# A kernel of attention and feed-forward: the order of all units of work as a written table in place of a list scheduler

## The chip, the cores and the metric

The kernel runs on one core of a Trainium2 chip. The metric is the device time of one execution in microseconds (us), the median of three runs. The engines are named as in the profile: PE (TensorE, products), PEld (its weight loads), DVE (VectorE), ACT (ScalarE), POOL (GpSimd), and SP (SyncE), which issues every DMA of this kernel.

## The reference

Clustered attention is followed by a feed-forward layer with a maximum of three branches. Four batches, 8 heads, 768 positions, 64 wide; 16 clusters; the layer is 512 to 768 to 512 for 3072 tokens, all in float32.

```python
q_assign = np.argmax(np.einsum('bhsd,hcd->bhsc', q_n, c_n), axis=-1)   # q_n, k_n, c_n: rows divided by their norm
k_assign = np.argmax(np.einsum('bhsd,hcd->bhsc', k_n, c_n), axis=-1)
mask = q_assign[:, :, :, None] == k_assign[:, :, None, :]
scores = np.where(mask, scale * np.matmul(q, k.transpose(0, 1, 3, 2)), -1000000000.0)
attn = softmax(scores)                       # maximum taken off, exp, divided by the sum
x = np.matmul(attn, v)                       # heads side by side: 3072 x 512
h = np.maximum(np.maximum(x @ w1, x @ w2), x @ w3)
out = h @ w_out
```

## The kernel before

Float32 values are split into a high and a low float16 part, so that a product of two such values is three products in float16. Heads go in pairs (4 pairs in each of 4 batches). The kinds of work are:

- *prep(b, pr)*: q and k of a pair are loaded (L678) into a stage buffer, scaled by a power of two that comes from their maximum (L684 or L686, then small DVE steps L692 to L715 and a small product, L702), and split (L753 to L761). Cluster scores (L734 in batch 0, L778 and L782 later) are transposed on DVE (L530), turned into one-hot rows (L533 to L579), and moved into the operands, so that one product gives the score and the mask.
- *v_first, v_prep*: the same for v (L838 to L904); the maximum over the partitions goes through a small product (L425).
- *weights*: w1, w2, w3 and w_out arrive as 64-bit numbers (wd, L961), are cast and shifted to float32 (L966 or L968, L972), scaled by their maximum (L1013), and split into w16a, w16b and wo (L983 to L989).
- *tile_units*: the 192 tiles of 128 queries by 768 keys: scores on PE (L1203, L1205) into a PSUM tile called big, row maximum on DVE (L1214), exponential on ACT (L1220), the split (L1223 or L1276, then L1226 or L1279), and the transposition of both parts by DMA (L1229). In the first 40 tiles every second one is transposed by PE instead (L1251, taken out by L1257 and L1259).
- *visit*: six tiles make a visit (three of each head); then the product with v (L1153). In batch 0 the sums are divided out afterwards: L1138, L1145, spread by ACT (L1168), multiplied by DVE (L1172) and split (L929 or L931, L1087).
- *ffn*: when the four pairs of a block of 384 tokens are there, 18 hidden products (L1335) of 12 matmuls, evictions with the maximum (L1347, L1349), splits (L929 or L931, L1087), then 3 output products (L1388), eviction and store (L1398, L1402).

A *unit* is one step of these kinds: a function that issues one or a few instructions on one engine. `Plan.add` collects 3117 of them with their dependences, their buffers (*leases*) and a priority. A unit whose engine is a dict (`pick`) may run on one of several: 640 units. `port=True` marks work on DVE which the scheduler keeps apart from work on POOL.

`Plan.run` of before is a list scheduler. It keeps a clock per engine, and takes on each free engine the ready unit of the lowest priority, moved by constants in NUDGE. For a `pick` unit it chooses the engine that would end first. The order in which units are taken is the order in which their instructions are issued, so it fixes the queue of every engine. Between engines, the framework puts the semaphores. All buffers of a tag come from one pool with `bufs` places.

```python
if u.pick and min(u.costs, key=lambda x: over(u, x)) != e:
    continue
late = max(u.at, when) + self.SAFE[e] > now
if rank is None or (late, u.prio, u.n) < rank:
    best, rank = u, (late, u.prio, u.n)
```

Of the kernel before, what the change touches and what calls it, by code (L numbers as in the profile page):

```python
# [8 lines left out]
F32 = mybir.dt.float32  # L9
# [13 lines left out]

class Lease:
    def __init__(self, plan, tag, make):
        self.tag, self.make, self.users, self.held, self.tile = tag, make, [], False, None
        plan.leases.append(self)

    def __call__(self):
        if self.tile is None:  # L30
            self.tile = self.make()
        return self.tile
# [12 lines left out]
class Plan:  # L45


    LAG = {"PE": 0.17, "DVE": 0.085, "ACT": 0.09, "POOL": 0.03, "SP": 0.0}
    SEM = 0.04
    LAND = 1.45  # L50
    RING = 2.6
    NEAR = 0.0
    SAFE = {"PE": 0.5, "DVE": 0.0, "ACT": 0.0, "POOL": 0.0, "SP": 0.0}
    BIAS = {"PE": 0.0, "DVE": 0.5, "ACT": 0.0, "POOL": 0.0, "SP": 0.0}

    def __init__(self, caps, ordered, nudge):
        self.units, self.leases, self.caps, self.ordered = [], [], caps, ordered
        self.nudge, self.part = nudge, None
# [4 lines left out]
    def add(self, eng, cost, fn, deps=(), leases=(), prio=0.0, tail=0.0, work=0.0, port=False):  # L63
        kind, *at = self.part or ("", 0)
        prio += self.nudge.get(kind, {}).get(tuple(at), 0.0)
# [12 lines left out]
    def run(self, nc):  # L78
        for n, u in enumerate(self.units):
            u.n, u.left = n, len(u.deps)  # L80
            u.at = 0.0
            for d in u.deps:
                d.next.append(u)
        queue = {}
        for x in self.leases:
            if x.tag in self.ordered:
                queue.setdefault(x.tag, []).append(x)
        for q in queue.values():
            q.sort(key=lambda x: min((u.prio, u.n) for u in x.users))
        place = {t: 0 for t in queue}  # L90
        freed = {t: [0.0] * c for t, c in self.caps.items()}
        for x in self.leases:
            x.left, x.done = len(x.users), 0.0
        ready = {e: [u for u in self.units if e in u.costs and not u.left] for e in self.LAG}
        free = {e: 0.0 for e in self.LAG}
        server = 0.0
        port, last = 0.0, "POOL"
        TURN = ["PE", "POOL", "DVE", "ACT", "SP"]
        now = 0.0
        win, busy, warm = 0, {}, False  # L100
        total = len(self.units)
        count = 0

        def can(u):
            when = u.at
            need = {}
            for x in u.leases:
                if x.held:
                    continue
                t = x.tag  # L110
                if t in queue and queue[t][place[t]] is not x:
                    return None
                need[t] = need.get(t, 0) + 1
            for t, k in need.items():
                f = sorted(freed[t])
                if len(f) < k:
                    return None
                when = max(when, f[k - 1])
            return when

        def over(u, e):
            out = max(free[e], now) + u.costs[e]
            if u.port and e == "DVE":
                out = max(out, port + u.costs[e])
            out += sum(
                x.costs[e] for x in ready[e] if x is not u and not x.pick and x.prio < u.prio + self.NEAR and x.at < now + 1.0
            )
            return self.BIAS[e] + (max(out, server) + u.work + self.LAND if e == "SP" else out + self.LAG[e])

        while count < total:  # L130
            soonest = None
            moved = False
            for e in self.LAG if last == "POOL" else TURN:
                if free[e] > now + 1e-9:
                    soonest = free[e] if soonest is None else min(soonest, free[e])
                    continue
                best, rank = None, None
                for u in ready[e]:
                    if rank is not None and (u.at + self.SAFE[e] > now, u.prio, u.n) >= rank:
                        continue  # L140
                    when = can(u)
                    if when is None:
                        continue
                    if e == "POOL" or e == "DVE" and u.port:
                        when = max(when, port)
                    if when > now + 1e-9:
                        soonest = when if soonest is None else min(soonest, when)
                        continue
                    if u.pick and min(u.costs, key=lambda x: over(u, x)) != e:
                        continue  # L150
                    late = max(u.at, when) + self.SAFE[e] > now
                    if rank is None or (late, u.prio, u.n) < rank:
                        best, rank = u, (late, u.prio, u.n)
                if best is None:
                    continue
                u = best
                moved = True
                u.eng, u.cost = e, u.costs[e]
                for x in u.costs:
                    ready[x].remove(u)  # L160
                for x in u.leases:
                    if not x.held:
                        x.held = True
                        if x.tag in queue:
                            place[x.tag] += 1
                        f = freed[x.tag]
                        f.sort()
                        f.pop(0)
                cost = u.cost
                if e == "PE":  # L170
                    w = int(now // 3.413)
                    while win < w:
                        share = busy.get(win, 0.0) / 3.413
                        warm = True if share > 0.5 else False if share < 0.25 else warm
                        win += 1
                    cost = cost if warm else 2 * cost
                    w = int(now // 3.413)
                    here = min(cost, (w + 1) * 3.413 - now)
                    busy[w] = busy.get(w, 0.0) + here
                    busy[w + 1] = busy.get(w + 1, 0.0) + cost - here  # L180
                if e == "SP":
                    out = max(now + cost, server - self.RING)
                    server = max(out, server) + u.work
                    free[e] = out
                    u.end = server + self.LAND
                else:
                    free[e] = now + cost
                    u.end = now + cost + self.LAG[e] + u.tail
                    if e == "POOL" or e == "DVE" and u.port:
                        port, last = now + cost, e  # L190
                if u.pick:
                    u.fn({"DVE": nc.vector, "ACT": nc.scalar, "POOL": nc.gpsimd, "SP": nc.sync}[e])
                else:
                    u.fn()
                u.fn = None
                count += 1
                for x in u.leases:
                    x.left -= 1
                    x.done = max(x.done, u.end)
                    if not x.left:  # L200
                        freed[x.tag].append(x.done + self.SEM)
                        x.tile = None
                for d in u.next:
                    d.left -= 1
                    d.at = max(d.at, u.end + self.SEM)
                    if not d.left:
                        for x in d.costs:
                            ready[x].append(d)
            if not moved:
                assert soonest is not None, "no unit can go on"  # L210
                now = soonest
# [3 lines left out]
def kernel(  # L215
# [48 lines left out]
    NUDGE = {  # L264
# [58 lines left out]
        },  # L323
        "wo": {
            (0,): 3.5, (1,): 1.5, (2,): 1.8, (3,): 7.4, (4,): 1.7, (5,): -1.2, (6,): 2.5,
        },
    }

    ctx.enter_context(tc.manual_schedule())
# [1125 lines left out]
```

## Time and profile before

| | |
|---|---|
| median of 3 runs | 729.19 us (728.7 to 730.13) |
| profiled execution | 729.67 us, its span 727.9 us |
| busy, PE | 669.1 us (92% of the span) |
| busy, DVE | 578.9 us (80%) |
| busy, ACT | 515.0 us (71%) |
| busy, POOL | 410.5 us (56%) |
| DMA moved | 121.03 MB, 166 GB/s on average |
| granted PE clock, mean | 0.964 |

The page cuts the span into 40 slices of 18.2 us; a digit is the busy share in tenths. A row of waits reads: engine and line that waited, what ended the wait, total us, how many times, longest. A row of a group reads: line, engine, operation, tiles out<-in, shapes, count; then busy us and mean ns of one; then idle time just ahead of it and what ended it. A row of a stretch gives for each engine its busy us and its count of instructions, then the granted PE clock, the share of the DMA engines, and GB/s.

### The profile page before, as it was taken

How to read it: one execution, taken by the hardware profiler on the slowest of the kernel's cores; microseconds unless marked ns; L12 is line 12 of the kernel's file. 1: busy time of each engine (PE TensorE's matmuls, PEld its weight loads, DVE VectorE, ACT ScalarE, POOL GpSimd, SP SyncE). 2: the span in 40 equal slices, each digit the busy share in tenths (PEclk: the TensorE clock that was granted, in tenths of full speed). 3: DMA queues.
4: the chain of work that ended last, by engine and by line, in shares of the span. 5: the costliest groups of instructions: out<-in, count | busy, mean ns of one | idle time of the engine just before them, and what ended most of it. 6: DMA issues, size and time to landing. Idle time of an engine off the chain costs nothing. (4 is left out here: it accounts for less than half of the span.)

```text
span 727.9 us, 13125 instructions
## 1 busy us (share of the span) xinstructions
PE 669.1 (92%) x4461; PEld 385.9 (53%) x4461; DVE 578.9 (80%) x1431; ACT 515.0 (71%) x888; POOL 410.5 (56%) x397
## 2 busy tenths in 40 slices
PE   2577768889899999999999999999999999999997
PEld 0234546555456555655556655565556655555563
DVE  7989788999988977999998877889898976763110
ACT  5877787987987767869578677888677777663211
POOL 3857777797755551577667542767658534540110
PEclk9668789999999999999999999999999999999999
DMA  8467777786999998799999888999998897676001
GB/s 307 142 142 178 181 180 178 169 200 124 201 207 196 213 155 184 134 199 189 216 215 212 176 152 166 170 188 208 203 231 143 132 169 153 124 115 140 15 0 44
DMA packets 297795, 121.03 MB, mean 166 GB/s; under 512 B 273024, under 2 KB 284160, under 8 KB 297728
## 3 DMA queue, kind: packets, MB, share of 16 engines
q1 hardware_dynamic: 297728, 120.20, 80.7%
q8 instruction: 35, 0.57, 0.3%
q14 instruction: 32, 0.26, 0.1%
HBM read 31.49 MB, written 6.29 MB: 52 GB/s over the span
## 5 line engine op out<-in xcount | busy, mean ns | idle before, releaser
L1214 DVE TENSOR_SCALAR_CACHE_REDUCE big<-big,nsc 128x768 f32<-128x768 f32 x192 | 192.3, 1017 | 12.1 <-PE big L1205 10.8
L1335 PE MATMUL one<-x,w16a 128*128 128x384 f16 x1152 | 197.4, 326 | 3.3 <-ACT vf_h L1347 2.4
L1335 PEld LDWEIGHTS <-w16a 128*128 128x128 f16 x1152 | 111.6, 98 | 78.9 <-issue 6.0
L1226 POOL TENSOR_TENSOR hl<-e,hl 128x768 f16<-128x768 f32 x71 | 118.5, 1672 | 38.6 <-ACT hl L1223 36.8
L1220 ACT ACTIVATE e<-big,nm 128x768 f32<-128x768 f32 x116 | 104.4, 901 | 30.8 <-DVE big L1214 19.1
L1203 PE MATMUL big<-qk 128*128 128x512 f16 (+1 forms) x384 | 97.1, 335 | 15.3 <-ACT e L1220 10.5
L1153 PE MATMUL big<-pt,v 128*64 128x384 f16 x1152 | 104.0, 336 | 5.9 <-ACT e L1220 3.3
L1335 PE MATMUL one<-x,w16b 128*128 128x384 f16 x576 | 99.5, 326 | 0.1
L1205 PE MATMUL big<-qk 96*128 96x512 f16 (+1 forms) x384 | 97.2, 335 | 0.0
L1270 POOL TENSOR_SCALAR e<-e,rs 128x768 f32<-128x768 f32 x53 | 49.3, 931 | 82.0 <-DVE rs L1241 55.4
L1153 PEld LDWEIGHTS <-v 128*64 128x64 f16 x1152 | 70.3, 113 | 38.8 <-issue 11.7
L1220 ACT ACTIVATE big<-big,nm 128x768 f32<-128x768 f32 x76 | 66.4, 874 | 34.2 <-DVE big L1214 27.7
L1223 ACT CAST hl<-e 128x768 f16<-128x768 f32 x96 | 79.3, 830 | 11.0 <-POOL e L1270 7.9
L1279 DVE SCALAR_TENSOR_TENSOR hl<-big,rs,hl 128x768 f16<-128x768 f32 x72 | 72.8, 1012 | 11.5 <-ACT hl L1276 11.3
L1335 PEld LDWEIGHTS <-w16b 128*128 128x128 f16 x576 | 55.6, 97 | 38.8 <-issue 2.4
L1276 ACT ACTIVATE hl<-big,rs 128x768 f16<-128x768 f32 x72 | 64.5, 898 | 12.6 <-ACT big L1220 4.5
L1203 PEld LDWEIGHTS <-qk 128*128 128x128 f16 x384 | 35.5, 99 | 47.0 <-issue 25.0
L1205 PEld LDWEIGHTS <-qk 96*128 96x128 f16 x384 | 38.5, 100 | 27.0 <-issue 2.5
L1087 POOL TENSOR_TENSOR wf_h<-wf_h 128x384 f16<-128x384 f32 x24 | 22.4, 934 | 52.6 <-ACT wf_h L929 52.0
L1349 DVE SCALAR_TENSOR_TENSOR wf_h<-one,wf_h 128x384 f32<-128x384 f32 x48 | 26.5, 552 | 32.0 <-PE one L1335 30.4
L1388 PE MATMUL one<-wo,vf_h 128*128 128x512 f16 x216 | 49.9, 388 | 0.6 <-DVE vpow L428 0.6
L1388 PE MATMUL one<-wo,wf_h 128*128 128x512 f16 x216 | 48.3, 379 | 0.0
(172 smaller groups left out, 1001.8 us busy)
## 6 DMA issues: line engine op xcount, KB each, us to landing
stage<-in_qk_dram SPq DMA_DIRECT2D x32, 384.0 KB, 4.7
wd<-in_moe_w_dram SPq DMA_DIRECT2D x18, 512.0 KB, 4.6
out_dram<-o SPq DMA_DIRECT2D x24, 256.0 KB, 2.8
qk<-qk SPq DMA_DIRECT2D x15, 384.0 KB, 4.2
qk<-qk SPq DMA_DIRECT2D x30, 192.0 KB, 4.0
stage<-in_v_dram SPq DMA_DIRECT2D x12, 384.0 KB, 5.3
wd<-in_moe_w_out_dram SPq DMA_DIRECT2D x6, 512.0 KB, 4.7
qk<-cl_t SPq DMA_DIRECT2D x60, 48.0 KB, 2.4
```

Of the source, the lines that this page charges most:

```text
L1153: nc.tensor.matmul(t()[D * i : D * i + D, 0:nb], v()[:, i, kt, a], pts[i % len(pts)]()[:, rows[i], c * QT + kt, :], start=(m == 0), stop=( ...
L1203: nc.tensor.matmul(t()[:, lo:hi], aq[:, qs], ak[:, lo:hi], start=True, stop=False)
L1205: nc.tensor.matmul(t()[:, lo:hi], bq[0:K2, qs], bk[0:K2, lo:hi], start=False, stop=True)
L1214: nc.vector.tensor_scalar(s, s, -SCALE if exact else nscs[:, b, pr : pr + 1], 3.0e38, op0=ALU.mult, op1=ALU.min, accum_out=nm())
L1220: nc.scalar.activation(e(), t()[:, 0:S], AF.Exp, bias=nm(), scale=-1.0, accum_out=r)
L1223: nc.scalar.copy(hl()[:, 0, :], e())
L1226: eng.tensor_tensor(hl()[:, 1, :], e(), hl()[:, 0, :], op=ALU.subtract)
L1270: eng.tensor_scalar(e(), e(), r(), 1.0, op0=ALU.mult, op1=ALU.mult)
L1276: nc.scalar.activation(hl()[:, 0, :], e(), AF.Copy, scale=r())
L1279: eng.scalar_tensor_tensor(hl()[:, 1, :], e(), r(), hl()[:, 0, :], op0=ALU.mult, op1=ALU.subtract)
L1335: nc.tensor.matmul(t()[:, 0:nb], w16[jt // JA][:, jt % JA, wa, i, ct], x16[b, gi, ct]()[:, xa, 0:nb], start=(m == 0), stop=(m == 3 * CT - 1),)
L1388: nc.tensor.matmul(t()[:, 0:DM], h16(jt)[:, ha, tt * P : (tt + 1) * P], wo16[0][:, jt, wa, :], start=(m == 0), stop=(m == 3 * JT - 1),)
```

## The change

The scheduler and its constants go. In their place stand two strings: ORDER has the numbers of all 3117 units in the order in which they are issued, and HANDS has one letter for each `pick` unit in the order of their numbers (V for DVE, S for ACT, G for POOL, Q for SP). `Plan.run` walks through the table. The table comes from a local search that moves single units. No unit is added or removed, and what a unit does is unchanged.

The buffers of a tag are no longer one pool tag with n places but n tags with one place each, `big.0`, `big.1`, `big.2`. The plan keeps a list of free places by tag; a lease takes the first of it when its first unit is issued, and puts it at the end when its last unit has been issued. The small columns of prep and mask_rows (`q_m`, `cl_m` and the like) hang on the place of their lease.

```diff
+ORDER = """
+1 0 18 19 52 51 2-5 7 6 8-13 153 417 155 14 15 20-23 30 24 16 17 54 53 39 25 55 26 29 56 40 27 57 63 58 28 41
...
+3102-3104 3108 3111 3109 3110 3056 3114 3112 3113 3115 3116
+"""
+
+HANDS = """
+VVVSSSGSGQQGSSGGSGQQGSSSGGGQQGSVSVGGGGSGSVGSGSSGSSGGGGVSSGGSGSSGSGSVGGGGSGSSGSGSVSSGSSVGGVSGGVSSGSGGSSGSGGVSGG
...
+"""
 class Lease:
...
     def __call__(self):
         if self.tile is None:
-            self.tile = self.make()
+            self.place = self.plan.places[self.tag].pop(0)
+            self.tile = self.make(self.place)
         return self.tile
...
     def run(self, nc):
...
+        engines = {"V": nc.vector, "S": nc.scalar, "G": nc.gpsimd, "Q": nc.sync}
+        hands = iter(HANDS.replace("\n", ""))
+        for u in self.units:
+            u.hand = engines[next(hands)] if u.pick else None
+            u.done = False
...
+        for n in order:
+            u = self.units[n]
+            assert all(d.done for d in u.deps)
             for x in u.leases:
...
+                x()
+            u.fn(u.hand) if u.pick else u.fn()
+            u.fn, u.done = None, True
+            for x in u.leases:
+                x.left -= 1
+                if not x.left:
+                    x.tile = None
+                    self.places[x.tag].append(x.place)
...
-    NUDGE = {
...
     def pool_lease(pool, tag, shape, dt, name=None):
-        return plan.lease(tag, lambda: pool.tile(shape, dt, tag=tag, name=name or tag, bufs=caps[tag]))
+        return plan.lease(tag, lambda i: pool.tile(shape, dt, tag=f"{tag}.{i}", name=name or tag, bufs=1))
...
-        u_t.append(add("SP", 1.43, tr, [u], [hl, pt], step, work=2.15))
+        u_t.append(add("SP", 1.43, tr, [u], [hl, pt], step, work=2.2))
```

The last line's `work` was an input of the scheduler's clock for SP; nothing reads it any more.

More of the change, by code (lines that the diff above doesn't have):

```diff
@@ L24 @@
+"""
 class Lease:
     def __init__(self, plan, tag, make):
-        self.tag, self.make, self.users, self.held, self.tile = tag, make, [], False, None
+        self.plan, self.tag, self.make, self.users, self.held, self.tile = plan, tag, make, [], False, None
         plan.leases.append(self)
@@ L45, with __init__ @@
 class Plan:
[L48 to L58, printed above, removed]
+    def __init__(self, caps):
+        self.units, self.leases = [], []
+        self.places = {t: list(range(n)) for t, n in caps.items()}
     def lease(self, tag, make):
@@ L78, in run @@
     def run(self, nc):
[L79 to L84, printed above, removed]
-        for x in self.leases:
[L86 to L106, printed above, removed]
-            for x in u.leases:
[L108 to L211, printed above, removed]
@@ new lines, in run @@
+        engines = {"V": nc.vector, "S": nc.scalar, "G": nc.gpsimd, "Q": nc.sync}
[3 more added lines that the diff above has]
+            u.done = False
+        for x in self.leases:
+            x.left = len(x.users)
+        order = []
+        for w in ORDER.split():
+            a, *z = map(int, w.split("-"))
+            order += range(a, z[0] + 1) if z else [a]
+        assert sorted(order) == list(range(len(self.units)))
@@ L408, in pow2_units @@
     def pow2_units(cols, p, prio, deps, later=None):
-        m = plan.lease("sc_m", lambda: sb.tile([P, 1], F32, tag="sc_m", name="sc_m", bufs=caps["sc_m"]))
-        s = plan.lease("sc_s", lambda: sb.tile([P, 1], F32, tag="sc_s", name="sc_s", bufs=caps["sc_s"]))
+        m = plan.lease("sc_m", lambda i: sb.tile([P, 1], F32, tag=f"sc_m.{i}", name="sc_m", bufs=1))
+        s = plan.lease("sc_s", lambda i: sb.tile([P, 1], F32, tag=f"sc_s.{i}", name="sc_s", bufs=1))
         a = one()
@@ L525, in cols @@
             if name not in mcol:
-                mcol[name] = sb.tile([P, n24], F32, tag=name, name=name, bufs=2)
+                ct()
+                mcol[name] = sb.tile([P, n24], F32, tag=f"{ct.tag}.{name}.{ct.place}", name=name, bufs=1)
             return mcol[name]
@@ L657, in prep @@
     def prep(b, pr):
-        plan.part = ("qk", b, pr)
         n0 = start[b, pr]
@@ L663, in prep @@
         xs = None if (b, pr) in RAW else [stage(b), stage(b)]
-        small = None if (b, pr) in RAW else plan.lease("q_s", lambda: {})
+        small = None if (b, pr) in RAW else plan.lease("q_s", lambda i: {"": i})
         t = qkt[b, pr] = pool_lease(sb, "qk", [P, 4, 2, S], F16)
@@ L673, in sm @@
             if name not in d:
-                d[name] = sb.tile([P, w], F32, tag=name, name=name, bufs=caps["q_s"])
+                d[name] = sb.tile([P, w], F32, tag=f"{name}.{d['']}", name=name, bufs=1)
             return d[name]
@@ L847, in v_first @@
     def v_first():
-        plan.part = ("v", 0)
         h = H // 2
@@ L868, in v_first @@
         for pr in range(NPAIR):
-            plan.part = ("v", 0, pr)
             prio = start[0, pr] + V_LEAD
@@ L883, in v_prep @@
     def v_prep(b, pr):
-        plan.part = ("v", b, pr)
         prio = start[b, pr] + V_LEAD
@@ L911, in v_common @@
     def v_common(b):
-        plan.part = None
         p, i = const([P, 1], F32, f"pv_{b}"), const([P, 1], F32, f"iv_{b}")
@@ L955, in piece @@
     def piece(src, prio, dst, dst_lease, conv_deps=()):
-        raw = plan.lease("wd", lambda: fp.tile([P, n512 + 1, 4], I16, tag="wd", name="wd", bufs=2))
-        tl = plan.lease("top", lambda: top)
+        raw = plan.lease("wd", lambda i: fp.tile([P, n512 + 1, 4], I16, tag=f"wd.{i}", name="wd", bufs=1))
+        tl = plan.lease("top", lambda i: top)
         def load():
@@ L995, in weights @@
         for jt in range(JT):
-            plan.part = ("w", jt)
             x = pool_lease(fp, "wf", [P, 3 * n512], F32)
@@ L1025, in weights @@
         for jt in range(JT):
-            plan.part = ("wo", jt)
             if jt % 3 == 0:
@@ L1032, in weights @@
             u = piece((w, 1), prio, part, x)
-            s = plan.lease("w_s", lambda: sb.tile([P, 1], F32, tag="w_s", name="w_s", bufs=caps["w_s"]))
+            s = plan.lease("w_s", lambda i: sb.tile([P, 1], F32, tag=f"w_s.{i}", name="w_s", bufs=1))
             row = worow[:, jt : jt + 1]
@@ L1057, in weights @@
             u_wo[jt] = [u_r, split16(part, x, s, s, hi, lo, [u] + u_raw, prio)]
-        plan.part = ("wo", JT)
         prio = W_0 + W_STEP * 24
@@ L1108, in visit @@
                 step += 1
-        plan.part = ("av", n)
         p = step + AV_PRIO
@@ L1187, in tile_units @@
     def tile_units(step, b, pr, i, qt, g, pt, at, rs, u_t, u_e, norm):
-        plan.part = ("tile", step)
         pool = by_pool(step) or step in BY_PE
@@ L1324, in ffn @@
         for jt in range(JT):
-            plan.part = ("hid", b, gi, jt)
             for i in range(3):
@@ L1376, in ffn @@
         ]
-        plan.part = ("out", b, gi)
         prio = max(k + (F_0 + F_SPAN) * (share if small else 1), W_0 + W_STEP * 25)
@@ L1381, in ffn @@
             t = one()
-            o = plan.lease("wd", lambda: fp.tile([P, DM], F32, tag="wd", name="o", bufs=2))
+            o = plan.lease("wd", lambda i: fp.tile([P, DM], F32, tag=f"wd.{i}", name="o", bufs=1))
             def outp(tt=tt, t=t):
```

55 lines of the change are left out of this document (25 added, 30 removed), and 151 rows, old and new, of tables (NUDGE, ORDER).

## The prediction

> **What bounds the kernel now.** I read the busy shares and the slices of the page first, then busy time by stretch, then who waits for whom on DVE and PE in the opening.
>
> ```profile
> PE 669.1 (92%) x4461; PEld 385.9 (53%) x4461; DVE 578.9 (80%) x1431; ACT 515.0 (71%) x888; POOL 410.5 (56%) x397
> ...
> PE   2577768889899999999999999999999999999997
> ...
> DVE  7989788999988977999998877889898976763110
> ...
> PEclk9668789999999999999999999999999999999999
> ```
>
> PE has full slices only from about the eleventh on, some 200 us in. Before that DVE is the fuller row. Busy time of each stretch (count, busy us per engine, granted clock, DMA share):
>
> ```profile
> 0.00:117.00 117.00, 74.16 (x434) 43.23 (x434) 98.49 (x209) 87.35 (x152) 74.53 (x93) 0.80 0.73 188
> 0.00:200.00 200.00, 149.37 (x965) 88.19 (x966) 178.41 (x407) 158.81 (x278) 141.59 (x157) 0.88 0.75 182
> 120.00:200.00 80.00, 72.21 (x513) 42.88 (x511) 77.05 (x191) 69.30 (x122) 65.31 (x62) 1.00 0.78 172
> 200.00:700.00 500.00, 495.78 (x3370) 285.19 (x3369) 397.72 (x1020) 351.63 (x603) 266.19 (x237) 1.00 0.88 168
> 700.00:728.00 28.00, 24.00 (x130) 12.53 (x128) 2.79 (x5) 4.58 (x8) 2.74 (x3) 0.99 0.08 29
> ```
>
> From 200 to 700 us PE idles 500 − 495.78 = 4.2 us, at the end 28 − 24.00 = 4.0. In the first 200 it idles 200 − 149.37 = 50.6. PE's work does not change in amount, so nearly all that an order can win lies before 200 us. There DVE is busy for 178.41, idle for 21.6: 117 − 98.49 = 18.5 up to the point where the fourth visit is multiplied out (L1172 at 117 us, which frees the first hidden layer), and 80 − 77.05 = 2.95 from 120 to 200. The first hidden layer needs four whole visits, so until then there is no spare PE work. DVE's queue, with its waits, sets the end of this opening, and PE's full stretch only moves with it. What DVE waits for from 0 to 120 us (total, times, longest), whole list:
>
> ```profile
> DVE xs L1172 <- PE big L1153: 4.1, 3, 2.0
> DVE pt L1259 <- ACT pt L1257: 3.0, 3, 1.9
> DVE big L1214 <- PE big L1205: 2.7, 5, 1.4
> DVE q_m L692 <- ACT qk L684: 1.8, 2, 1.3
> DVE wf L972 <- ACT top L966: 1.7, 1, 1.7
> DVE sq L460 <- DMA c_sb<-in_centroids_dram: 1.7, 1, 1.7
> DVE warm L442 <- PEq L1443: 0.8, 1, 0.8
> DVE cwf L506 <- ACT cw L495: 0.4, 1, 0.4
> DVE vp L428 <- PE one L425: 0.4, 1, 0.4
> DVE big L1214 <- ACT e L1220: 0.3, 1, 0.3
> DVE c_yr L469 <- ACT c_y L464: 0.3, 1, 0.3
> ```
>
> The sum is 17.2 us. The start (centroids 1.7, warm 0.8, cwf 0.4, c_yr 0.3: 3.2) stays in any order; 14.0 is waits in mid-queue, which another unit put ahead could fill. And PE's waits from 0 to 200 us, longest rows:
>
> ```profile
> PE one L425 <- DVE sc_m L415: 12.8, 3, 10.8
> PE big L1203 <- ACT e L1220: 10.0, 8, 2.5
> PE one L480 <- DVE c L475: 5.6, 1, 5.6
> PE big L1251 <- ACT e L1220: 5.5, 7, 1.6
> ```
>
> The 10.8 us stall is PE held at the small product of the values' maximum, with the cluster scores of a pair queued behind it.
>
> **The change part by part.** The table and the 640 letters give every one of the 3117 units its place and engine. I compare queue by queue, by unit number, with what the scheduler of before emits.
>
> *PE's queue.* The same 473 units; 275 places hold another unit, on average 0.97 places from where it stood, 7 at most; the last eleven hidden products and three output products are the same. So the tail from 700 us costs or wins 0, and of the 4.2 us in the middle I take 0 as well (ends −2 and +2, half of it refilled or doubled). In the opening the cluster scores of pair (0,2) now stand ahead of the product that waited 10.8 us. PE is not the bound there, so the worth is what DVE gets earlier to fill its waits with (below); by itself 0.
>
> *Which engine.* 166 units change: POOL to ACT 54, POOL to DVE 42, ACT to POOL 34, DVE to POOL 28, DVE to ACT 7, ACT to DVE 1. Prices:
>
> ```profile
> L1226 DVE TENSOR_TENSOR hl<-e,hl 128x768 f16<-128x768 f32 x25 | 24.9, 995 | 4.6 <-ACT hl L1223 4.0 <-issue 0.3
> L972 DVE SCALAR_TENSOR_TENSOR wf<-wd,top 128x512 int32<-128x512 int32 x24 | 18.8, 783 | 1.7 <-ACT top L966 1.7
> L1013 DVE TENSOR_REDUCE wmx<-wf 128x1 f32<-128x1536 f32 x6 | 10.5, 1742 | 0.0
> L842 DVE TENSOR_TENSOR v<-stage,v 128x768 f16<-128x768 f32 x1 | 1.5, 1526 | 0.0
> L686 DVE TENSOR_REDUCE q_m<-stage 128x1 f32<-128x768 f32 x14 | 13.1, 942 | 0.1
> ```
>
> And from the view of the line L761 alone, shortest, median and longest in ns:
>
> ```profile
> L761 DVE TENSOR_TENSOR qk<-stage,qk x8: 945/950/2172, 41.8 to 535.7; 128x768 f16<-128x768 f32 x8
> ```
>
> Ahead of the fourth L1172 DVE loses one L972 (0.78), two L1226 (1.99) and an L761 (0.95 to 2.17), and gains two L842 and an L1226: 3.7 to 4.9 out; in, 2 × 1.53 + 0.99 = 4.1, or 3.0 if the L842 run at the 0.99 of the same shape. Between −1.9 and +0.4: I take 0. Ahead of the eighth L1172, the last of batch 0, out are four L686 (3.8), four L1226 (4.0) and three L761 (2.9 to 6.5); in are four L1226 and three L842 (7.0 to 8.6) and five half-size ones (2 to 3, half to two thirds of 0.99): −5 to +1, and I take 0 again, as both queues hold 380 units there. POOL has 101 units instead of 123 ahead of that point. ACT gets 116 instead of 103 units ahead of the fourth visit's spread (L1168): at the mean of the first stretch, 87.35 / 152 = 0.57 us, 7.5 us, against 117 − 87.35 = 29.7 us in which it idles there. It is cover, not cost, as long as ACT's own waits shrink.
>
> *DVE's order.* Here lies the gain; each wait of the list by what now stands ahead. Before the first L1172 a weight maximum (L1013, 1.74 us) and an L972 (0.78) are pulled ahead, and the third stands ten places later: of 4.1 I take 3. The first L1259 goes back eight places, the second seven, the fourth four, each with whole 1 us units put between: of 3.0 I take 2. L1214 waits for PE, which is no longer held up for 10.8 us: 1.3 of 2.7. L972's wait is a cast's that changes engine: half, 0.9. L692 gets 0.5 of 1.8, since what passes it at 10 us must itself wait for PE. Sum 7.7. New waits can come in their place: their bounds are 0 and the whole 7.7; I take 0.7, as most of the filled places have slack behind them. Net −7.0.
>
> *SP's queue.* The loads of pair (0,2) go ahead of the first weight load; they need a stage place that the first four loads hold, so the weight load queues behind them.
>
> ```profile
> POOL top L968 <- DMA wd<-in_moe_w_dram: 6.9, 2, 5.6
> ```
>
> That is the price if the cover goes: 5.6 us on POOL. The first L972 stands 63rd in DVE's queue and the L968 is ACT's now; I take 0 and keep +2 as an end.
>
> *Buffer places by turns.* A tag of three buffers becomes three tags of one, and the place that was freed first is handed out. The framework's allocator already did that: for the tag big it gave another place in 3 of 260 cases. What a place can cost shows in the row above in which L1203 waits for L1220, 10.0 us in 8 times: that is a PSUM place coming free. It lies on PE while PE is not the bound, so 0; ends −2 and +2.
>
> **Sum.** The profiled execution took 729.67 us, of which 727.9 are the span. 727.9 − 7.0 = 720.9; the median of the runs, 729.19, stands 0.5 under the profiled one. 729.19 − 7.0 = 722.2, and I forecast 722.
>
> **The rivals.**
> *More (711 to 717).* All 14.0 us of mid-queue waits and the 2.95 of 120 to 200 fall away: 729.2 − 17 = 712. For it: POOL and ACT have idle time to take work into. Against it: several waits are true chains (L1172 needs its product).
> *The waits come back elsewhere (726 to 731).* DVE is 96% busy from 120 to 200; if units pulled ahead only push those that the later visits need, or ACT with its 13 more units becomes late, the opening ends where it ended: 729.
> *Slower: DVE and POOL collide.* The old scheduler held a two-input unit of DVE back while it thought POOL busy (port=True); the table looks at nothing at run time. The price of a collision is in the L761 row: 2.17 against 0.95, 1.2 us. Ahead of the eighth L1172, 81 such units of DVE stand in the table, 76 before. Six more hits than before cancel the gain; twelve, one unit in seven, give 729.2 − 7 + 14.6 = 737. Against it: POOL has 22 units fewer ahead of that point, so fewer chances to meet. The Trainium skill states the rule in "GPSIMD Engine Reference", "Key points": POOL shares its SBUF interfaces with DVE and contends with DVE instructions that read two SBUF inputs. By that rule the L842 and L1087 moved to DVE are exposed and L1214, which reads PSUM, is not; the 2172 of L761 and the 1526 of the one L842 agree.
>
> **How the numbers follow.** Forecast (717 to 726) 0.50; more 0.15; waits come back 0.18; slower by collisions (731 to 740) 0.15; rest 0.02. The likeliest gives 722. From 712 to 731 leaves some 0.2 out, mostly above. A measurement here can't tell less than about 0.2%, 1.5 us, from no change: faster 0.50 + 0.15 + 0.10 of the third case = 0.75, same 0.07, slower 0.18.
>
> **What would show it.** Right: DVE's idle time from 0 to 117 us falls from 18.5 to about 11; its waits at L1172 and L1259 shrink; the first L1335 begins near 112 us, not 119; PE's busy time in 200 to 700 stays at 495 or more; the end is cut by what the opening gained. Wrong: L761, L842 and L972 on DVE grow in their mean (collisions); ACT shows new waits ahead of L1168; PE's idle time after 200 us exceeds 10 us; or DVE's time in 0 to 200 falls without PE's full stretch beginning earlier.

## The result, and the profile after

The changed kernel takes 713.1 us (median of 4 runs, 712.89 to 714.27) against 729.62 us of the kernel before on the same chip (4 runs, 728.7 to 730.13): a ratio of 0.9778 with an interval of [0.9761, 0.9795], 16.5 us less. The forecast was 722 (712 to 731), 7 us less. The direction is right, but the gain is more than twice the one forecast: the time lies outside the forecast's own 717 to 726 and within 711 to 717, where the rival "more" stood.

The profiled execution of the changed kernel took 713.19 us, its span 711.4. Its line numbers are 34 to 44 smaller: L1172 is L1130, L1335 is L1291, L1214 is L1171, L1259 is L1216, L972 is L934, L692 is L658, L1226 is L1183. In the kernels with extra instructions they are six larger than that. Its page, busy shares and slices:

```profile
PE 666.8 (94%) x4461; PEld 384.1 (54%) x4461; DVE 570.9 (80%) x1439; ACT 531.4 (75%) x920; POOL 380.6 (53%) x363
...
PE   4578788998999999999999999999999999999997
...
DVE  7989989999998866999899777999899977782120
...
PEclk9678879999999999999999999999999999999999
```

The opening of PE (the slices before its full stretch) is denser. Busy time of each stretch, changed kernel:

```profile
0.00:117.00 117.00, 83.08 (x481) 46.08 (x481) 105.04 (x227) 99.80 (x175) 74.07 (x94) 0.82 0.77 196
0.00:200.00 200.00, 160.60 (x1053) 93.10 (x1054) 185.99 (x440) 176.55 (x311) 135.28 (x151) 0.90 0.81 194
120.00:200.00 80.00, 75.00 (x548) 45.10 (x549) 77.95 (x204) 73.75 (x132) 59.55 (x56) 1.00 0.85 190
200.00:700.00 500.00, 498.68 (x3376) 287.77 (x3374) 384.90 (x1000) 352.91 (x608) 245.28 (x213) 1.00 0.85 162
```

DVE now idles 117 − 105.04 = 12.0 us up to 117 us, where it was 18.5, and issues 227 instructions there instead of 209. PE idles 200 − 160.60 = 39.4 us in the first 200 (50.6 before) and 500 − 498.68 = 1.3 from 200 to 700 (4.2 before). The span of 16.5 us less is made of 11.2 and 2.9 of PE's idle time in these two stretches and 669.1 − 666.8 = 2.3 of its busy time, under 0.1 us being left to the end. The last term is no gain by itself: with the same products PE's busy time lies anywhere from 661.1 (e11) to 672.4 us (e14) in the profiles of the next section.

What DVE waits for from 0 to 120 us, changed kernel, whole list (total, times, longest):

```profile
DVE big L1171 <- PE big L1162: 4.2, 9, 1.3
DVE sq L426 <- DMA c_sb<-in_centroids_dram: 1.6, 1, 1.6
DVE big L1171 <- ACT rs L1093: 1.3, 1, 1.3
DVE cl_t L497 <- PE big L700: 1.1, 1, 1.1
DVE warm L408 <- PEq L1398: 0.8, 1, 0.8
DVE cwf L472 <- PE one L446: 0.7, 1, 0.7
DVE wf L934 <- POOL top L930: 0.4, 1, 0.4
DVE xs L1130 <- PE big L1111: 0.3, 1, 0.3
DVE c_yr L435 <- ACT c_y L430: 0.3, 1, 0.3
```

The sum is 10.7 us, and 7.3 without the start, where 14.0 were. And the longest rows of PE's waits from 0 to 200:

```profile
PE big L1160 <- ACT e L1177: 7.2, 7, 1.7
PE big L1160 <- DVE pt L1216: 5.3, 5, 1.9
PE one L446 <- DVE c L441: 5.2, 1, 5.2
PE big L700 <- DMA stage<-in_qk_dram: 4.8, 2, 2.9
PE one L391 <- DVE sc_m L381: 3.3, 3, 1.5
```

The 10.8 us at the small product (now L391) are gone; PE waits for places of big, as before. When the opening ends is read from the view of the line L1172, whose last start column is the eighth multiplication, the last of batch 0. Before, and the changed kernel:

```profile
L1172 DVE TENSOR_TENSOR xs<-big,xs x8: 540/558/560, 61.1 to 211.4; 128x384 f32<-128x384 f32 x8
```

```profile
L1130 DVE TENSOR_TENSOR xs<-big,xs x8: 544/552/558, 57.4 to 198.4; 128x384 f32<-128x384 f32 x8
```

The first comes 3.7 us earlier, the eighth 13.0. Between them lies the first hidden product (first start in the view of L1335, and of L1291):

```profile
L1335 PE MATMUL one<-x,w16a x1152: 322/326/337, 119.0 to 700.3; 128*128 128x384 f16 x192
```

```profile
L1291 PE MATMUL one<-x,w16a x1152: 323/326/337, 109.9 to 683.9; 128*128 128x384 f16 x192
```

9.1 us earlier; its last is 16.4 earlier. For DVE's queue ahead of the fourth and of the eighth multiplication I summed the durations of the units that stand there. Ahead of the fourth: 98.5 busy and 18.6 idle before, 96.1 and 11.9 after. Ahead of the eighth: 188.1 and 23.3 before, 184.4 and 14.0 after. So of the 13.0 us at the eighth, 9.3 are idle time and 3.7 are shorter or moved work.

These are single profiles, and the runs of the next section show how far they vary. With the changed opening the eighth multiplication comes at 198.1 (e4), 198.4 (above) and 199.3 us (e10), with the old one at 211.4 (above), 211.8 (e5), 212.7 (e1) and 213.8 (e9). A single row of waits varies more: the one at L1130, 0.3 above, is 1.8 in e4 and 2.0 in e10. The clock granted to PE is not the cause of the 13 us: from 0 to 200 us it was 0.88 before and 0.90 in the changed kernel, but also 0.90 in e1, with the old table, and 0.93 in e10, which is later than the changed kernel.

### The profile page after: what moved, and what is told of

Same layout as the page of the kernel before. It is cut to its first block, busy times and chain, and to the rows that moved or that the text cites. A ratio compares the mean times of both kernels' runs of the same rounds, so it can differ in the third digit from the quotient of the medians.

```text
span 711.4 us, 13113 instructions
## 1 busy us (share of the span) xinstructions
PE 666.8 (94%) x4461; PEld 384.1 (54%) x4461; DVE 570.9 (80%) x1439; ACT 531.4 (75%) x920; POOL 380.6 (53%) x363
## 5 line engine op out<-in xcount | busy, mean ns | idle before, releaser
L1171 DVE TENSOR_SCALAR_CACHE_REDUCE big<-big,nsc 128x768 f32<-128x768 f32 x192 | 192.8, 1017 | 20.3 <-PE big L1162 18.6
L1291 PE MATMUL one<-x,w16a 128*128 128x384 f16 x1152 | 197.4, 326 | 0.2 <-ACT xs L1126 0.2
L1183 POOL TENSOR_TENSOR hl<-e,hl 128x768 f16<-128x768 f32 x80 | 133.4, 1670 | 70.3 <-ACT hl L1180 62.6
L1291 PEld LDWEIGHTS <-w16a 128*128 128x128 f16 x1152 | 111.8, 98 | 76.0 <-issue 1.9
L1160 PE MATMUL big<-qk 128*128 128x512 f16 (+1 forms) x384 | 98.6, 340 | 14.5 <-ACT e L1177 7.2
L1111 PE MATMUL big<-pt,v 128*64 128x384 f16 x1152 | 100.2, 327 | 1.4 <-DVE hl L1183 0.5
L1291 PE MATMUL one<-x,w16b 128*128 128x384 f16 x576 | 98.9, 326 | 0.1
L1162 PE MATMUL big<-qk 96*128 96x512 f16 (+1 forms) x384 | 98.5, 338 | 0.3 <-DVE qk L567 0.3
L1111 PEld LDWEIGHTS <-v 128*64 128x64 f16 x1152 | 67.5, 110 | 32.0 <-issue 8.5
L1227 POOL TENSOR_SCALAR e<-e,rs 128x768 f32<-128x768 f32 x44 | 40.4, 919 | 80.3 <-DVE rs L1198 70.9
L1236 DVE SCALAR_TENSOR_TENSOR hl<-big,rs,hl 128x768 f16<-128x768 f32 x72 | 72.9, 1013 | 11.4 <-ACT hl L1233 10.6
L1291 PEld LDWEIGHTS <-w16b 128*128 128x128 f16 x576 | 55.9, 98 | 37.9 <-issue 1.1
L727 POOL TENSOR_TENSOR qk<-stage,qk 128x768 f16<-128x768 f32 x27 | 44.4, 1653 | 12.5 <-ACT qk L724 11.9
L1343 PE MATMUL one<-wo,vf_h 128*128 128x512 f16 x216 | 48.1, 379 | 0.6 <-ACT o L1353 0.6
L1305 DVE SCALAR_TENSOR_TENSOR wf_h<-one,wf_h 128x384 f32<-128x384 f32 x48 | 26.5, 553 | 25.8 <-PE one L1291 24.4
```

The lines of the kernel that those rows point to most:

```text
L727: eng.tensor_tensor(t()[:, AQ, i], x(), t()[:, BQ, i], op=ALU.subtract)
L1111: nc.tensor.matmul(t()[D * i : D * i + D, 0:nb], v()[:, i, kt, a], pts[i % len(pts)]()[:, rows[i], c * QT + kt, :], start=(m == 0), stop=( ...
L1160: nc.tensor.matmul(t()[:, lo:hi], aq[:, qs], ak[:, lo:hi], start=True, stop=False)
L1162: nc.tensor.matmul(t()[:, lo:hi], bq[0:K2, qs], bk[0:K2, lo:hi], start=False, stop=True)
L1171: nc.vector.tensor_scalar(s, s, -SCALE if exact else nscs[:, b, pr : pr + 1], 3.0e38, op0=ALU.mult, op1=ALU.min, accum_out=nm())
L1183: eng.tensor_tensor(hl()[:, 1, :], e(), hl()[:, 0, :], op=ALU.subtract)
```

## The experiments

All are the changed kernel with another table or with a few added instructions. "Span" is that of one profiled execution, to be set beside 711.4 (changed) and 727.9 (before).

**Which part of the change: e1, e2, e3.** Only the tables differ.

```diff
-ORDER, HANDS: changed kernel
+e1: order before, engines before     (places by turns alone are left)
+e2: order before, engines after
+e3: order after,  engines before
```

> The order and the engines that the scheduler of before emits, written as a table into the changed kernel; only the handing out of buffer places by turns is left of the change. If the order makes the gain: 729 to 730 us, as before. If the places by turns make a part of it (a score tile's PSUM place comes free earlier): 727 or less, and the waits of the score products for the exponential in 0 to 200 us fall from 10.0 towards the 7.2 us of the changed kernel.

> Order of before, engines of the changed kernel (166 units run on another engine, each at the point of the issue order where it stood). If the gain is mainly load taken off POOL and collisions that fall away (3.7 us of DVE's busy time ahead of the eighth L1172): 722 to 727 us. If engines and order only work together: 729 to 735, since the moved units stand in front of others on their new queue and wait there for their inputs.

> Order of the changed kernel, engines of before. If the order fills DVE's waits by itself (9.3 us of idle time ahead of the eighth L1172, and 3.4 us of PE's idle time later): 716 to 721 us. If engines and order only work together: 726 or more, with DVE's idle time ahead of the eighth L1172 above 20 us.

e1 took 728.87 us, ratio 1.0008 [0.9994, 1.0021]: places by turns are worth nothing. e2 took 757.79, ratio 1.0403 [1.0384, 1.0422], and e3 778.3, ratio 1.0679 [1.0653, 1.0706]. Both are far beyond what I expected of them. Waits of DVE that grew, up to the eighth multiplication, in e2, then in e3:

```profile
DVE xs L1130 <- PE big L1111: 7.6, 3, 3.8
DVE q_m L658 <- ACT qk L650: 6.8, 4, 2.4
```

```profile
DVE vf_h L1305 <- POOL vf_h L1046: 6.9, 2, 6.1
```

Before, the first two are 4.8 and 1.8 us up to that point, and the third is not there. DVE's idle time ahead of the eighth L1130 rises from 23.3 to 39.5 us in e2 and 39.1 in e3, with 188.9 and 191.3 us of work (188.1 before). I take it that a unit which goes to another engine while the order stays stands at the wrong place of that engine's queue, and what is behind it is late; this was not followed unit by unit here (e15 below is one such case). POOL's largest rows do not tell it: its waits at L1183 for ACT are 67.9 us in e2, but 62.6 in the changed kernel too. So the gain cannot be split into one of the order and one of the engines.

**Which stretch: e4, e5, e6.** The table is changed up to a point and the old one follows, or the reverse.

```diff
-ORDER, HANDS: changed kernel
+e4: after's first 976 entries (to the eighth L1172), then before's order and engines
+e5: before's first 986 entries (to the same point), then after's
+e6: after's first 88 entries (to the first score tile), then before's
```

> Order and engines of the changed kernel up to and with the eighth L1172 (the first 976 entries of the table), then those of before for all units that are left. If the gain of the opening (13.0 us at that step) and of the rest (3.4 us) add up independently: 716 to 717.5 us. If the rest depends on the table as a whole, so that the old order after a new opening makes PE wait: over 719.

> The mirror of the previous split: order and engines of before up to and with the eighth L1172 (986 entries), then the changed table for what is left. If opening and rest add up: 3.4 us under before, 725 to 726.5 us, with PE's idle time after 212 us near 13 us less its tail. If the rest can only be used behind the new opening (its queue places assume units that come earlier): 729 or more.

> The changed table only up to the first score tile (88 entries), which began 4.3 us earlier in the changed kernel; then the order and engines of before. If DVE's queue is one chain through the opening, so that a gain at its head is carried on: 724 to 726 us, first tile near 23 us. If the early gain is swallowed by later waits in the old order: 728 to 730 us though the first tile is early.

e4 took 716.7 us, ratio 0.9838 [0.9823, 0.9854]; its eighth multiplication is as early as in the changed kernel:

```profile
L1130 DVE TENSOR_TENSOR xs<-big,xs x8: 542/552/558, 56.1 to 198.1; 128x384 f32<-128x384 f32 x8
```

That is 13.3 us earlier than before, and it is 13.2 ahead at the last output product: the opening's gain is carried to the end untouched. e5 took 728.15, ratio 0.9984 [0.9966, 1.0002], span 726.0: the rest by itself is worth 1 to 2 us, at the edge of what can be told. e6 took 730.16, ratio 1.0019 [1.0006, 1.0033]. It begins its first score tile 4.4 us earlier, and has lost this by the fourth multiplication (118.2 us, before 117.1). DVE's waits up to 120 us in e6, longest rows:

```profile
DVE xs L1130 <- PE big L1111: 4.8, 3, 1.8
DVE pt L1216 <- ACT pt L1214: 4.5, 3, 1.9
DVE q_m L658 <- ACT qk L650: 2.7, 1, 2.7
```

An early start alone comes back as waits at the places of DVE's queue that the old order left unfilled. This is the rival "the waits come back elsewhere", true of this part of the table and not of the whole.

**What bounds the opening, and what bounds the rest: e7, e8, e10, e9.** Work that nobody needs is added behind units of one engine: six reductions of 1.2 us on DVE between 46 and 100 us (e7) or between 301 and 390 us (e10), thirty small copies of 0.2 us on ACT between 45 and 105 us (e8); and the six of e10 behind the same units in the old table (e9).

```diff
+EXTRA = {1018: 1, 144: 1, 204: 1, 1074: 1, 311: 1, 1158: 1}   # e7; other numbers in e8, e10, e9
...
+            for _ in range(EXTRA.get(n, 0)):
+                nc.vector.tensor_reduce(self.scr, self.one, axis=AX.X, op=ALU.max)   # e8: nc.scalar.copy
```

> The changed kernel with six more DVE reductions (1024 float16 each, into an unused column, about 1.1 us each, 6.6 us together) between 45 and 105 us. If DVE's queue sets the end of the opening: 4.5 to 7 us above the changed kernel's 713, that is 717.5 to 720. If DVE's remaining 12 us of idle time there take them in: under 715.

> The changed kernel with 30 more small ACT copies (16 columns, some 0.2 us each, 6 us together) between 45 and 105 us. If DVE alone sets the pace of the opening: 713 to 715 us, since ACT idles 17 us there. If ACT, 85% busy in the first 117 us, has become as tight as DVE: 717 to 720.

> The same six DVE reductions, put between 300 and 400 us. If PE alone bounds that part: 712.5 to 714 us, nothing lost. If the score tiles wait there for DVE too (DVE is 91% busy in that stretch): 715 or more.

> The table of before with the same six DVE reductions, at the same units as in the run with six late reductions (300 to 381 us here). If the tightness of DVE after 200 us is new, made by the changed order: 729 to 731 us. If the order of before was as tight there, so that PE's 98 to 99% never was a cover: 735 to 738.

e7 took 720.41, ratio 0.9883 [0.9857, 0.9908], span 717.4, 6.0 above the changed kernel. Its multiplications:

```profile
L1136 DVE TENSOR_TENSOR xs<-big,xs x8: 542/548/557, 59.2 to 204.7; 128x384 f32<-128x384 f32 x8
```

The eighth is 6.3 us later; ahead of it DVE is busy 6.5 longer and idle 13.8 instead of 14.0. So DVE's work in the opening counts nearly one for one (6.3 for 7.2 us added), and the 14 us of waits that are left cannot be filled by just any unit at these places. e8 took 713.85, ratio 0.9771 [0.9742, 0.98]: 6.5 us of ACT cost nothing that shows in the median. Its profile is that of the slowest of its four runs (span 713.3); the eighth multiplication is 1.7 us later there, and 0.9 later in e10 without any added ACT work. ACT is cover there, or nearly, as the prediction took it.

e10 took 721.42, ratio 0.9894 [0.9868, 0.992], span 719.5. It is 8.1 us above the changed kernel, where PE was thought to be the only bound. The stretch from 300 to 400 us in the changed kernel, then in e10:

```profile
300.00:400.00 100.00, 99.77 (x691) 58.42 (x689) 90.78 (x244) 79.42 (x135) 62.72 (x54) 1.00 0.97 190
```

```profile
300.00:400.00 100.00, 93.96 (x633) 53.60 (x632) 97.06 (x237) 74.91 (x127) 58.51 (x50) 1.00 0.89 179
```

PE loses 5.8 us of work in that stretch although DVE idled 9.2 us of it. The same six in the old table, e9: 733.37 us, ratio 1.0053 [1.0034, 1.0072], span 731.5, 3.6 us above before, between the two expectations. Before, then e9:

```profile
300.00:400.00 100.00, 98.42 (x679) 56.73 (x680) 91.39 (x245) 76.83 (x133) 71.74 (x62) 1.00 1.01 203
```

```profile
300.00:400.00 100.00, 96.59 (x668) 55.40 (x667) 93.71 (x241) 75.03 (x129) 70.88 (x60) 1.00 0.98 195
```

The six start at 312.9 us in e9, and the last lies behind this stretch. How late each of the 192 row maxima (L1171) is against the kernel without the added work separates their cost from what stood there already. In e10 they are 0.8 us late ahead of the first reduction and 8.1 behind the last: 7.3 us for 7.2 of work. In e9 they are 2.4 late ahead of the first, though the table up to there is the old one, 4.2 behind the last, and the kernel ends 3.6 late: 1.2 to 1.8 us for the same work. The medians differ less, 8.3 us against 4.3; how much of the 4.3 is the spread of the opening stays open. So PE has nearly the same busy share in both kernels, but by the traces the changed order leaves DVE no room in this stretch and the old one did. The Trainium skill, "Perfetto Trace Analysis", "Identifying the Most-Contended Engine", has one optimise the engine with the highest occupancy, and warns that matmul busy time is no measure of distance to the limit; here the 99.77 of PE did not say that DVE at 90.78 was free.

**The stall of 10.8 us: e11.** The cluster scores of pair (0,2) (unit 97) go back behind the product of the values' maximum (unit 160) on PE.

```diff
-47 48 66 97 160 989 161 107
+47 48 66 160 97 989 161 107
```

> The changed kernel with one unit moved: the cluster scores of pair (0,2) go back behind the product of the values' maximum on PE, the order of before. If that stall is worth what PE's row says: up to 10 us. If it matters only as far as it holds the scores' own inputs (their load lands at 17 to 20 us, the product is free at 23): the scores are 2 to 3 us later, 713 to 716 us.

715.57 us (712.41 to 716.02), ratio 0.9802 [0.9778, 0.9826], its span 710.6. PE's wait is back:

```profile
PE one L391 <- DVE sc_m L381: 12.9, 4, 10.0
```

The first score tile begins at 25.8 us instead of 23.1, yet the eighth multiplication comes at 197.5, no later than in the changed kernel. The profile is that of the fastest of the four runs; the other three took 715.5 to 716.0, and the interval of the ratio overlaps the changed kernel's. So the longest row of PE's waits was worth 0 to 2.5 us and not 10, since DVE and not PE set the end of the opening.

**Six units from DVE to POOL: e12, then split as e15 and e16.** If DVE's work counts one for one, work taken from it should gain. Four low parts of v (L842; units 166, 169 in the first batch, 462, 747 later) and two low parts of weights (L988; units 276, 279) change their letter and keep their place.

```diff
-HANDS: V at units 166, 169, 276, 279, 462, 747
+HANDS: G at the same units            (e12: all six; e15: 166, 169; e16: the other four)
```

> The changed kernel with six letters changed from DVE to POOL: three L842 of the opening and one at 363 us, and two low parts of w16 (L988), all needed only 20 us or more later. It takes 5.1 us of DVE's busy time out of the first 200 us and 1.2 later. If DVE's busy time counts one for one: 707 to 709.5 us. If POOL's longer instructions (1.6 us) collide with DVE's two-input ones and give the time back: 712.5 to 715, with L972 on DVE longer than now.

> The changed kernel, with only the two first low parts of v (units 166 and 169, L842) moved from DVE to POOL, at their places. Theory 1 (POOL's queue is held: the second of them waited 5.5 us for ACT's cast of v, with the low parts of three exponentials, L1226, behind it): nearly all of the 7.3 us that the six moved units cost come from these two: 718 to 721. Theory 2 (the six on POOL stretch DVE's two-input instructions, each alike): a third of it, 714.5 to 716.

> The changed kernel, with the other four of the six (two L842 of batch 1, two L988) moved from DVE to POOL, at their places. Theory 1 (POOL's queue is held by the early two): these four lie where POOL waits for nothing long, so DVE wins up to 3 us of work: 710 to 713.5. Theory 2 (stretching of DVE's two-input instructions): two thirds of the 7.3: 717 to 719.

e12 took 720.81, ratio 0.9887 [0.987, 0.9903], span 718.7: 7.3 us slower in the span, although units worth some 5.1 us of DVE's time in the first 200 us have left it. e15 took 716.69, ratio 0.9819 [0.9806, 0.9833], span 715.1; e16 716.51, ratio 0.9809 [0.9786, 0.9833], span 714.7. Each carries about half (3.7 and 3.3), so neither of the two theories holds with its time. In e15 the longest wait of POOL that the changed kernel did not have, and the multiplications:

```profile
POOL v L808 <- ACT v L804: 5.5, 1, 5.5
```

```profile
L1130 DVE TENSOR_TENSOR xs<-big,xs x8: 543/554/559, 61.2 to 202.4; 128x384 f32<-128x384 f32 x8
```

The low part of v sits at the head of POOL's queue and waits 5.5 us for ACT; behind it stand the low parts of the exponentials. The first multiplication is 3.8 us later, the eighth 4.0, and 3.7 are still there at the end. The Trainium skill states in "PSUM — Partial Sum Buffer", "Engine vs sequencer instructions", that the queues of ScalarE, VectorE and GpSimd are strict first in, first out; the 5.5 us agree. In e16 there is nothing of the kind in the opening: the eighth multiplication is 0.4 late. There DVE's own instructions grow. Groups of lines on DVE, 0 to 200 us, the changed kernel, then e16:

```profile
L934 DVE SCALAR_TENSOR_TENSOR wf<-wd,top 128x512 int32<-128x512 int32 x24 | 18.0, 752 | 0.5 <-POOL top L930 0.5
L1183 DVE TENSOR_TENSOR hl<-e,hl 128x768 f16<-128x768 f32 x5 | 4.8, 966 | 0.0
```

```profile
L934 DVE SCALAR_TENSOR_TENSOR wf<-wd,top 128x512 int32<-128x512 int32 x24 | 19.5, 812 | 0.7 <-POOL top L930 0.7
L1183 DVE TENSOR_TENSOR hl<-e,hl 128x768 f16<-128x768 f32 x5 | 5.8, 1161 | 0.0
```

These two groups take 2.5 us more, as much as the three early units were worth, while DVE ahead of the eighth multiplication is busy only 0.2 us less. The growth is in single instructions beside POOL: an L934 at 125.2 us takes 1644 ns (676 in the changed kernel) and an L1183 at 126.8 takes 1912 (946), both while the two low parts of weights, now on POOL, run there (125.1 to 127.8 us).

The larger part of e16's loss comes later: PE's busy time from 200 to 700 us falls from 498.68 to 496.84. The row maxima (L1171) are 1.7 us late from 223 to 361 us, and 3.3 from 402 us on. The 1.3 between the eighth multiplication and 223 us was not followed. In the later step lies the fourth moved unit. Waits of POOL and of ACT from 350 to 390 us in e16:

```profile
POOL v L808 <- ACT v L804: 3.1, 1, 3.1
```

```profile
ACT e L1177 <- POOL hl L1183: 2.5, 1, 2.5
```

The low part of v waits at the head of POOL's queue for ACT, the low part of an exponential (L1183) stands behind it, and the next exponential waits for that one (0.2 us in the changed kernel). It is e15's case once more: 1.6 of e16's 3.3 us are a held queue.

**The single fillings of the prediction: e13, e14.** One weight maximum back behind the first L1172 (e13); twelve units back behind the first two L1259 (e14).

```diff
-... 184 185 1029 ... 203 1030 186 187
+... 184 1029 ... 203 1030 185 186 187                                        (e13)
-... 1002 994 111 1008 ... 112 181 80 1014 123 1006
+... 1002 994 78 178 96 79 110 1008 ... 80 1006 111 112 181 1014 123          (e14)
```

> The changed kernel, with one weight maximum (unit 185, 1.74 us on DVE), which it has ahead of the first L1172, put back behind it. My step of the prediction (it fills a wait for the product): DVE waits that long for the product of the first visit, 1.7 us more at L1172, and the opening ends 1 to 2 us later: 714 to 715. Rival (the waits are only redistributed; DVE's work in the opening counts, and where it stands does not): 712.5 to 713.5.

> The changed kernel, with twelve small and middle units of DVE (7 ahead of the first L1259, 5 ahead of the second, 5.6 us together) put back behind these two, as they stood before. My step of the prediction: the 3.0 us of waits for ACT's copy at L1259 come back to 2 of it, and the opening ends 2 us later: 715. Rival as in the run beside it (position inside the queue does not count): 713. A third possibility is that the first tiles go out earlier and it gets faster, 711 to 712.

e13 took 715.15, ratio 0.9798 [0.9785, 0.9811], span 713.3. The row of the wait, against 0.3 us in the changed kernel (1.8 and 2.0 in e4 and e10, which have the same opening), and the multiplications:

```profile
DVE xs L1130 <- PE big L1111: 2.9, 2, 2.1
```

```profile
L1130 DVE TENSOR_TENSOR xs<-big,xs x8: 541/552/558, 56.1 to 200.4; 128x384 f32<-128x384 f32 x8
```

The wait is longer, the eighth multiplication 2.0 us later, and the span 1.9 longer. But the wait is not all of it: DVE's idle time ahead of the eighth grows by 1.0 us (15.0; 14.0 in the changed kernel, 14.4 in e4, 14.7 in e10), and its busy time by another 1.0, because an L1183 at 90.5 us, beside two L950 on POOL, takes 1908 ns, where the longest in the changed kernel, e4 and e10 takes 1043 to 1047. So at most half of the 2.0 us is the step of the prediction; the other half is a meeting with POOL. e14 took 715.06 (711.73 to 716.71), ratio 0.9791 [0.9769, 0.9813]; its profile is that of the slowest of five runs, span 714.9. Its waits:

```profile
DVE xs L1130 <- PE big L1111: 2.0, 3, 1.5
DVE pt L1216 <- ACT pt L1214: 1.9, 2, 1.4
```

The 1.9 us at L1216 are back, as the step said; neither the changed kernel nor e4 or e10 has this row. The 2.0 at L1130 are no more than in e10. The eighth multiplication comes at 202.2, 3.8 later, and DVE's idle time ahead of it is 16.8 us, more than in all three. The trace bears the step out. The times by themselves do not settle it, as the runs spread over 5 us and the intervals overlap that of the changed kernel; the same holds, more narrowly, of e13's.

## Why the prediction was right in kind and wrong in size

The gain is 9.5 us larger than the net −7.0. The steps that failed are terms put at 0 or left out: DVE's content up to the eighth multiplication, taken as 0, measured −3.7; its waits between the fourth and the eighth, not in the sum, −2.6; the kernel behind the opening, taken as 0, −3.5. DVE's idle time up to the fourth, where the forecast stood, measured −6.7.

*What bounds the opening: right.* DVE's queue sets its end. Six added reductions cost nearly their length (e7), 30 ACT copies at most 1.7 us (e8), and the PE stall of 10.8 us at most 2.5 (e11).

*The waits, −7.0: right in sum for its stretch, less so one by one.* The list up to 120 us went from 17.2 to 10.7, less 6.5; its mid-queue part from 14.0 to 7.3. By the prediction's items: L1172 gave 3.8 (3 forecast; 2.3 and 2.1 if e4 and e10 are set in its place), L1259 3.0 (2), L692 1.8 (0.5), L972 1.3 (0.9), and L428 0.4 that I had not counted. New is 1.1 at L497 (0.7 forecast as new). L1214 has the wrong sign: I let it lose 1.3 because PE would no longer be held up; it grew from 3.0 in two rows to 5.5 (4.2 in e4, 4.8 in e10). Removing a wait of PE did not make PE's score products early for DVE. DVE's idle time to 117 us came to 12.0 (about 11 forecast).

*Stopping the account of the waits at 120 us: a term left out.* DVE also idled less behind that point: 9.3 us fewer ahead of the eighth multiplication, 6.7 of them ahead of the fourth. The 2.95 us of 120 to 200 appeared in the sum only within the rival "more". That is 2.6 us.

*DVE's content, taken as 0 twice: mis-sized.* Ahead of the fourth multiplication it is −2.4, beyond the bound of −1.9; ahead of the eighth −3.7, within −5 to +1. I had weighed only the swapped units. These gave 11.8 out and 10.6 in, 1.2 us. Of the rest, 2.0 us come from lines that have the same count on DVE in both kernels and ran shorter in sum; some 0.5 is overlap between records. The clearest case is a copy, the group before (0 to 200 us) and its line in the changed kernel:

```profile
L600 DVE COPY qk<-cl_t 32x768 f16<-32x768 f16 x4 | 3.0, 755 | 0.1
```

```profile
L567 DVE COPY qk<-cl_t x4: 351/352/354, 22.7 to 23.9; 32x768 f16<-32x768 f16 x4
```

Four times 0.40 us, 1.6; L972 is next, 783 to 752 ns in 24. It is no chance of one profile: the mean is 752 to 755 ns in all four profiles with the old opening (before, e1, e5, e9) and 352 in e4 and e10. Before, the three long copies (974, 966 and 730 ns, from 24.4 us on) lie beside L877 and L842 of POOL; in the changed kernel POOL runs nothing beside the last three.

*The rest of the kernel, taken as 0 (ends −2, +2): beyond the end.* At the eighth multiplication the gain is 13.0, at the end 16.5, so 3.5 us come from behind it: PE's idle time from there to the end falls from 7.5 to 5.2 us, its busy time from 508.9 to 507.8. By e5 that rest gives 1 to 2 us by itself, and e4 lacks 3.3 without it. The sentence "PE's full stretch only moves with it" fails here: e10 shows that in the changed kernel DVE's work counts in full behind a full row of PE, so order and content could still win or lose time where I allowed for neither. I read PE's 495.78 of 500 as a sign that nothing else counts. Which units win the 3.5 us no run isolates.

The sum, from the queue of DVE: −6.7 waits and −2.4 content to the fourth multiplication, −2.6 and −1.3 to the eighth, −3.5 behind: −16.5. Up to the eighth multiplication this is bookkeeping, as each start on DVE is the busy and idle time ahead of it; that the shift there is carried to the end is measured (13.3 and 13.2 us in e4, 6.3 and 6.0 in e7, 4.0 and 3.7 in e15).

*Places by turns, 0: right* (e1). *SP's queue, 0: not isolated.* POOL's wait for the weight load, which was to show the price, fell from 6.9 to this, in 0 to 200 us:

```profile
POOL top L930 <- DMA wd<-in_moe_w_dram: 2.3, 2, 1.8
```

DVE's wait behind it, at L934, is 0.4 in the list above: the cover held.

*The rivals.* "More" had the right time (712) by another sum: half of its waits stay, and content and rest that it did not count make up for them. "The waits come back" is what e6 does, and what e2 and e3 do many times over; the whole table avoids it. The collisions are real: e16 has them at 2.5 us for two groups of lines, e13 at 1.0 for one instruction. The changed kernel seems to have fewer than before: the lines with the same count ran 2.0 us shorter, L761 does not appear on DVE any more up to 200 us, and POOL is busy 135.28 us there instead of 141.59. I had counted how many DVE units are exposed; what POOL runs beside them at that moment decided in the cases followed here. POOL's units ahead of the eighth multiplication were also miscounted: its instructions there went from 162 to 149, 13 fewer and not 22. The rule of the Trainium skill in "GPSIMD Engine Reference", "Key points", speaks against more two-input units on DVE only as long as POOL runs beside them; e16 agrees with it: L934 and L1183 both read two operands in SBUF, and the two that met POOL took 1644 and 1912 ns instead of 676 and 946.

## What to carry to other kernels

In a kernel with in-order queues, find the one queue that sets the end of a stretch and count its busy and its idle time up to the last unit that the next stretch needs, not to the end of the waits that catch the eye: what comes late there stays late to the end (e4, e7, e15), while the longest wait of another engine may be worth little (e11). Order and engines of units are one choice: moving a unit to a less busy engine without finding it a new place in that queue lost 7 us where it should have gained (e12), and 29 and 50 us were lost when 166 units stood on engines that the order was not made for (e2, e3). A full row of one engine is no proof that the others are cover; add a known amount of work to them, and compare how late the kernel is just ahead of the added work with how late it is just behind it, since single profiles differ by 1 to 2 us before it begins (e9, e10).

## What was not expected of the hardware

- DVE's instructions of one kind and shape took up to twice as long under one table as under the other: the copy of 32x768 took 755 ns on average before and 352 after, and the sums of these differences are of the size of the changes that a table makes (2.0 us in the gain, 2.5 in e16).
- Six DVE reductions of 1.2 us from 301 to 390 us delayed the kernel by 7.3 us, their whole 7.2, with DVE idle 9.2 us of that stretch's 100 and PE 99.77% busy without them; under the old table the same six cost 1.2 to 1.8 in the trace.
